# Chunked attention and two gated MLPs: attention and the second MLP's weight conversions spread at one distance into the last plain block, with the stores of weight high halves

## Chip, cores and metric

The kernel runs on one core of one Trainium2 chip. The metric is the device time in microseconds of one execution; lower is better.

## What is computed

Inputs are float32. Attention works in chunks of 64 tokens, then come two gated MLPs, the second behind an RMS norm. Its core:

```python
scores = scale * np.matmul(q_c, k_c.transpose(0, 1, 2, 4, 3))   # per chunk of 64 tokens
attn = np.exp(scores - np.max(scores, axis=-1, keepdims=True))
attn = attn / (np.sum(attn, axis=-1, keepdims=True) + 1e-09)
out = np.matmul(attn, v_c)                                      # 8 x 8 heads x 576 x 64
x = out.transpose(0, 2, 1, 3).reshape(4608, 512)
x = (silu(x @ w_gate) * (x @ w_val)) @ w_out                    # 512 -> 1536 -> 512
rms = np.sqrt(np.mean(x * x, axis=-1, keepdims=True) + 1e-06)
xn = x / rms * rms_g
out = (silu(xn @ w2_gate) * (xn @ w2_val)) @ w2_out
```

## The kernel before

**Precision.** Every float32 operand of a large product is split into a high part (rounded to the matmul's type) and a low part, and three matmuls make a product (`mm3`, L625): high by high, high by low, low by high. Weights arrive as words that are taken apart: `rebase` (two ScalarE steps, L124 and L131) and `to_f32` (two VectorE steps, L140 and L145) make a float32 tile.

**Stages.** The 4608 tokens are 36 tiles of 128. The first MLP runs 3584 tokens as seven plain blocks (0 to 6) of 512, and the last 1024 as a superblock that saves an eighth of its products by Strassen-Winograd sums; the second MLP is five such superblocks. A plain block has 12 iterations, one for each slice f of 128 hidden columns, 84 in all, numbered here from 0: block j has iterations 12j to 12j+11. An iteration issues on TensorE 12 matmuls for the gate (`emit_g`), 12 for the value (`emit_v`), 12 for the output of the slice before (`emit_y`). ScalarE takes the tanh and rounds the hidden slice (hh); VectorE makes the two products (sg) and the low part (hl). Gate and value have one PSUM bank each, so the next gate waits for the product that read the last one.

**Positions.** Everything else is hung between these by a table. An iteration n has three positions, 3n, 3n+1 and 3n+2: behind the gate, value and output matmuls. `put(l, j, pos, fn)` hangs a function on a position, and each engine runs its work in the order of issue. `NP` is 36, the positions of a block. For attention tile i (8 to 35) with a = `score_at(i)`: scores are made at a by `att_both(i-1)`, which issues the value matmuls of tile i-1 with them; `att_m` (maximum, 16 exponentials with sums) at a+1, `att_n` (reciprocal on VectorE, scaling on GpSimd) at a+2, `att_td` (eight VectorE transposes each) at a+3 and a+4, `trans_att(i+1)` (VectorE transposes of the next tile's q and k) at a+2. q and k come in groups of some two tiles, in four-row pieces that `spread` issues on SyncE over 11 positions.

**Conversions.** The second MLP's weights are converted in plain blocks 1 to 5: every 6 positions one slice of `w2` (load at +1, `rebase` at +4, `to_f32` at +6). With every second slice the Winograd sums of the pair follow on GpSimd (`comb_add`, `comb_rest`), ScalarE (`comb_cast`), and stores (`comb_keep`). Gate and value pairs and `LATE` = 2 of six output pairs are done so; the other four pairs are done by `late_o` in the first two superblocks: at steps 26 and 47 of the first (a step is one of the 84 pairs of kt products of its gate and value phase), and at 20 and 41 of the second. The first MLP's own sums for its superblock are made by `whole` and `first_add` in blocks 1 to 5, and `whole` also stores the high half of the weight. Low halves of the first MLP's weights are loaded anew in each block from ScalarE's queue (`load_lo`, `load_lo_o`, L191 and L198).

**Superblocks.** A superblock has six groups (fp) of 84 matmuls for gate and value and then an output phase; its weights come through a ring of 16 tiles (`load_ring`), its inputs through `x_load` and `x_prep`. `y_out` adds, transposes on VectorE and stores a quarter ("11", "22", "21", "12") of the output in pieces.

## Time and profile before

| | |
|---|---|
| median of 3 runs | 1817.12 us (1816.77 to 1818.37) |
| profiled execution | 1817.92 us, span 1816.1 us |
| TensorE busy | 1738.8 us, 96% |
| VectorE busy | 1278.0 us, 70% |
| ScalarE busy | 811.6 us, 45% |
| GpSimd busy | 548.9 us, 30% |
| DMA | 392.86 MB, mean 216 GB/s |

In the profile PE is TensorE, PEld its weight loads, DVE VectorE, ACT ScalarE, POOL GpSimd and SP SyncE. A name with q (SPq) is an engine's sequencer, which issues DMAs. An arrow in an instruction's name reads output <- inputs; in a wait, who waited <- what ended the wait. TensorE's busy share is an average over stages: 96% says little of a single block, for which the windows below are cut at the first gate matmul of a block.

### The profile page before, as it was taken

Reading aid. Unit: us, or ns where it says so; the run is one execution under the profiler, and the core shown is the slowest. Engines: PE = TensorE matmul, PEld = TensorE weight load, DVE = VectorE, ACT = ScalarE, POOL = GpSimd, SP = SyncE. Lnnn points to the kernel's source line nnn. Section 1 sums busy time; section 2 is a strip of 40 time slices with the busy share of each in tenths; the row PEclk is TensorE's granted clock in tenths of the full one; section 3 lists DMA queues with packets and bytes.
Section 4 is the critical chain, followed back from the end, with each engine's and each line's share of the span. In section 5 each row is a group of like instructions: output and inputs, shape, how many; then the busy total and the mean of one; then the engine's idle time right before and its main releaser. Section 6 shows DMA issues by size and latency. Waiting matters only on the chain.

```text
span 1816.1 us, 29440 instructions
## 1 busy us (share of the span) xinstructions
PE 1738.8 (96%) x9978; PEld 1452.0 (80%) x9978; DVE 1278.0 (70%) x2232; ACT 811.6 (45%) x1902; POOL 548.9 (30%) x527
## 2 busy tenths in 40 slices
PE   7998989999898999999999999999999999999998
PEld 5786777777776787888777777888888888999998
DVE  6985666777765768556879777874695569569566
ACT  6862433444334344334546444533462345345343
POOL 1003446556555474213351643110021011002000
PEclk9998999999999999999999999999999999999999
DMA  9994777778777777354673779687668767987986
GB/s 243 314 240 113 196 207 210 219 206 232 212 199 219 214 206 230 99 184 129 200 228 103 213 220 336 182 259 233 194 208 248 211 195 211 293 270 252 303 253 166
DMA packets 462533, 392.86 MB, mean 216 GB/s; under 512 B 278576, under 2 KB 334640, under 8 KB 462384
## 3 DMA queue, kind: packets, MB, share of 16 engines
q1 hardware_dynamic: 444368, 346.74, 65.5%
q10 hardware_dynamic: 18016, 44.24, 7.8%
q8 instruction: 80, 1.31, 0.3%
q14 instruction: 69, 0.57, 0.1%
HBM read 310.90 MB, written 79.95 MB: 215 GB/s over the span
## 4 chain that ended last, share of the span: by engine, by line
PE 60%; DVE 16%; DMA 11%; ACT 5%; issue 3%; SPq 3%; POOL 2%; ACTq 0%; DVEq 0%; POOLq 0%
DVE pT L536 4%; DMA l<-lo_scratch 3%; SPq L438 2%; PE g L626 2%; PE g L627 2%; PE g L628 2%; PE v L626 2%; DMA w64g<-in_moe_w_gate_dram 2%; ACT p L492 2%; PE v L628 2%; PE v L627 2%; DMA lo<-lo_scratch 1%; PE ygA L627 1%; PE ygA L628 1%; PE ygA L626 1%
## 5 line engine op out<-in xcount | busy, mean ns | idle before, releaser
L1073 POOL TENSOR_TENSOR h<-h,h 128x512 f32<-128x512 f32 (+1 forms) x36 | 46.4, 1290 | 526.3 <-DVE h L1051 526.3
L626 PE MATMUL g<-xh,wg 128*128 128x512 f32 x336 | 136.8, 407 | 21.1 <-DVE sg L639 19.2
L1109 DVE TENSOR_TENSOR hp<-h,hp 128x512 fp32r<-128x512 f32 (+1 forms) x216 | 147.3, 712 | 6.0 <-ACT hp L1108 5.9
L536 DVE STREAM_TRANSPOSE pT<-p 32x128 f32<-32x128 f32 x448 | 135.6, 303 | 16.1 <-POOL p L520 9.9
L1031 ACT ACTIVATE sig<-sgt 128x512 f32<-128x512 f32 (+1 forms) x108 | 64.5, 598 | 184.0 <-DVE sgt L1039 183.9
L1108 ACT CAST hp<-h 128x512 fp32r<-128x512 f32 (+1 forms) x216 | 121.6, 584 | 53.9 <-PE yvA L628 21.1
L626 PE MATMUL v<-xh,wv 128*128 128x512 f32 x336 | 134.0, 399 | 9.1 <-DVE sg L655 8.1
L970 POOL TENSOR_TENSOR xf<-xf,xf 128x512 f32<-128x512 f32 (+1 forms) x48 | 80.4, 1676 | 196.3 <-DVE xo0l L966 68.5
L1032 DVE TENSOR_TENSOR sgt<-sgt,sig 128x512 f32<-128x512 f32 (+1 forms) x108 | 73.7, 683 | 86.8 <-ACT sig L1031 86.8
L627 PE MATMUL g<-xl,wg 128*128 128x512 f32 x336 | 133.3, 397 | 0.4 <-DVE xl L620 0.4
L628 PE MATMUL g<-xh,l 128*128 128x512 f32 x336 | 133.4, 397 | 0.0
L520 POOL TENSOR_TENSOR p<-p,r 128x512 f32<-128x512 f32 x36 | 42.1, 1168 | 300.3 <-DVE r L519 279.0
L660 DVE TENSOR_TENSOR hl<-sg,hh 128x512 fp32r<-128x512 f32 x84 | 75.5, 899 | 81.1 <-ACT hh L658 80.7
L628 PE MATMUL v<-xh,l 128*128 128x512 f32 x336 | 131.1, 390 | 0.0
L627 PE MATMUL v<-xl,wv 128*128 128x512 f32 x336 | 131.0, 390 | 0.0
L658 ACT CAST hh<-sg 128x512 fp32r<-128x512 f32 x84 | 51.8, 616 | 156.6 <-DVE sg L655 147.5
L626 PEld LDWEIGHTS g<-xh,wg 128*128 128x128 f32 x336 | 64.5, 192 | 43.4 <-DVE sg L639 27.7
L639 DVE SCALAR_TENSOR_TENSOR sg<-sg,g 128x512 f32<-128x512 f32 x84 | 57.3, 682 | 48.2 <-ACT sg L638 47.9
L626 PEld LDWEIGHTS v<-xh,wv 128*128 128x128 f32 x336 | 63.0, 188 | 26.3 <-DVE sg L655 12.1
L638 ACT ACTIVATE sg<-g 128x512 f32<-128x512 f32 x84 | 50.1, 596 | 73.7 <-PE g L628 73.4
L627 PE MATMUL y<-hl,wo 128*128 128x512 f32 x168 | 68.8, 409 | 12.5 <-DVE hl L660 12.1
L1051 DVE TENSOR_TENSOR h<-h,sgt 128x512 f32<-128x512 f32 (+1 forms) x108 | 74.4, 689 | 3.7
(858 smaller groups left out, 5277.5 us busy)
## 6 DMA issues: line engine op xcount, KB each, us to landing
wrg<-w_scratch SPq DMA_DIRECT2D x210, 256.0 KB, 3.7
wrv<-w_scratch SPq DMA_DIRECT2D x210, 256.0 KB, 3.6
wro<-w_scratch SPq DMA_DIRECT2D x210, 256.0 KB, 3.2
l<-lo_scratch ACTq DMA_DIRECT2D x54, 512.0 KB, 4.3
lo<-lo_scratch ACTq DMA_DIRECT2D x60, 256.0 KB, 4.8
w64g<-in_moe_w_gate_dram SPq DMA_DIRECT2D x19, 512.0 KB, 5.1
w64v<-in_moe_w_val_dram SPq DMA_DIRECT2D x19, 512.0 KB, 4.6
w_scratch<-wsg SPq DMA_DIRECT2D x18, 512.0 KB, 3.1
```

What stands on the lines that cost most here:

```text
L536: nc.vector.transpose(out=pT[o:o + 32, :, r:r + 32], in_=pt[r:r + 32, :, z, b * 32:b * 32 + 32])
L626: nc.tensor.matmul(o, sh, mh, start=first, stop=False, skip_group_check=free)
L627: nc.tensor.matmul(o, sh, ml, start=False, stop=False, skip_group_check=free)
L628: nc.tensor.matmul(o, sl, mh, start=False, stop=last, skip_group_check=free)
L639: return sg, lambda: nc.vector.scalar_tensor_tensor(out=sg[:, :n], in0=sg[:, :n], scalar=1.0, in1=g[:, :n], op0=ALU.add, op1=ALU.mult)
L660: return product, lambda: nc.vector.tensor_sub(hl[:, :n], sg[:, :n], hh[:, :n].bitcast(F32))
L970: nc.gpsimd.tensor_sub(o, a, b)
L1031: nc.scalar.activation(sg[:, :tw], src[:, :tw], AF.Sigmoid)
L1032: nc.vector.tensor_mul(t[:, :tw], src[:, :tw], sg[:, :tw])
L1051: nc.vector.tensor_mul(h[:, :tw], src[:, :tw], sgt[pos][:, :tw])
L1108: nc.scalar.copy(hh[:, :tw], src)
L1109: nc.vector.tensor_sub(hl[:, :tw], src, hh[:, :tw].bitcast(F32))
```

## The change

- Attention tiles come every 7 positions instead of 6.75 on the average, conversions every 7 instead of 6. So the last tile's value matmuls stand at position 232, in iteration 77, instead of 225, in iteration 75; the last conversion's sums reach position 230.
- `rebase` stands 4 positions behind its load instead of 3, `trans_att` of the next tile at a+5 instead of a+2, and the pieces of a q and k group start 3 positions later.
- The high halves are stored by `high_keep` in block 6, in 36 stores at positions 0 to 23, instead of by `whole` in blocks 1 to 5.
- `LATE` is 1: a fifth output pair goes to the superblocks; the first now has three, at steps 10, 31 and 52.
- The input of the first superblock is prepared from iteration 79 on, two pieces at each position, instead of from iteration 77, four at the end of each iteration.
- The RMS sums of a block are made at other positions, other tiles stand last, held stores are let go at two of three steps instead of one of two, and half of the "21" stores of the last superblock go out from ScalarE's queue.

```diff
--- before.py
+++ after.py
@@ -200,7 +200,7 @@
 
     flat = {}
     NP2 = NF // 2
-    LATE = 2
+    LATE = 1
     HK = KD * P // 2
     comb = {}
 
@@ -266,6 +266,9 @@
         h = whi[0, nm, f]
         nc.gpsimd.tensor_add(t, h.bitcast(F32), low_of(0, j, chunk(j, f), nm).bitcast(F32))
         flat[0, nm, f] = t
+
+    def high_keep(nm, p, side):
+        h = whi[0, nm, 2 * p + side]
         ks = [(k, c) for k, (which, c) in enumerate(PLAIN[nm]) if which == side]
         k, c, n = ks[0][0], ks[0][1], len(ks)
         nc.sync.dma_start(
@@ -308,7 +311,7 @@
 
     NCH = NT // CH
     SC = S // CH
-    last = [33, 34, 35, 12, 13, 22, 23, 24]
+    last = [12, 13, 22, 23, 32, 33, 34, 35]
     home = [i for i in range(NT // P) if i not in last] + last
     order = [home.index(i) for i in range(NT // P)]
 
@@ -794,7 +797,7 @@
             put(l, j, pos + z, lambda z=z: step(z))
 
     def score_at(i):
-        return NP + 27 * (i - 8) // 4
+        return NP + 7 * (i - 8)
 
     for i in range(NW // P, NT_):
         j = order[i] * P // NW
@@ -806,11 +809,11 @@
                 put(0, 0, a, lambda: att_both(7))
                 put(0, 0, a - 1, lambda: trans_att(8))
             put(0, 0, a + 1, lambda i=i: att_m(i))
-            if i + 1 < NT_:
-                put(0, 0, a + 2, lambda i=i: trans_att(i + 1))
             put(0, 0, a + 2, lambda i=i: att_n(i))
             put(0, 0, a + 3, lambda i=i: att_td(i, 0))
             put(0, 0, a + 4, lambda i=i: att_td(i, 1))
+            if i + 1 < NT_:
+                put(0, 0, a + 5, lambda i=i: trans_att(i + 1))
             put(0, 0, e, lambda i=i: att_both(i))
             put(0, 0, e + 1, lambda i=i, j=j: att_lo(i, j))
         else:
@@ -827,7 +830,7 @@
             g = where[c][0]
             if g > 0 and c == groups[g][-1] and g + 2 < len(groups):
                 if i > 8:
-                    dq, dv, nq, nv = score_at(i - 1) + 3, score_at(i + 1) + 1, 11, 4
+                    dq, dv, nq, nv = score_at(i - 1) + 6, score_at(i + 1) + 1, 11, 4
                 else:
                     dq, dv, nq, nv = {4: (20, 17, 9, 3), 6: (29, 38, 8, 4), 8: (38, 44, 11, 4)}[i]
                 spread(0, 0, dq, nq, lambda g=g: load_qk(g + 2))
@@ -838,9 +841,10 @@
             put(0, j, 3 + 2 * d, lambda pj=pj, d=d: rms_sq(pj, d))
         put(0, j, 13, lambda pj=pj: rms_cast(pj))
         put(0, j, 14, lambda pj=pj: rms_split(pj))
-        put(0, j, 17, lambda pj=pj: rms_mm(pj))
-        put(0, j, 20, lambda pj=pj: rms_mul(pj))
-        put(0, j, 22, lambda pj=pj: rms_newton(pj))
+        mm = (17, 17, 17, 16, 20, 19)[j - 1]
+        put(0, j, mm, lambda pj=pj: rms_mm(pj))
+        put(0, j, mm + 2, lambda pj=pj: rms_mul(pj))
+        put(0, j, mm + 4, lambda pj=pj: rms_newton(pj))
         for d in range(KD):
             put(0, j, 24 + 2 * d, lambda pj=pj, d=d: rms_x(pj, d))
             put(0, j, 26 + 2 * d, lambda pj=pj, d=d: rms_keep(pj, d))
@@ -849,13 +853,13 @@
 
     w2 = [(nm, f) for nm, m in (("g", NP2), ("v", NP2), ("o", LATE)) for fp in range(m) for f in (fp, fp + NP2)]
     for x, (nm, f) in enumerate(w2):
-        pos = NP + 6 * x
+        pos = NP + 7 * x
         put(0, 0, pos + 1, lambda nm=nm, f=f: load_w64(1, nm, f))
-        put(0, 0, pos + 4, lambda nm=nm, f=f: rebase(1, nm, f))
-        put(0, 0, pos + 6, lambda nm=nm, f=f: to_f32(1, nm, f))
+        put(0, 0, pos + 5, lambda nm=nm, f=f: rebase(1, nm, f))
+        put(0, 0, pos + 7, lambda nm=nm, f=f: to_f32(1, nm, f))
         if f >= NP2:
             for d, fn, kk in COMB:
-                put(0, 0, pos + d, lambda fn=fn, nm=nm, f=f, kk=kk: fn(nm, f - NP2, kk))
+                put(0, 0, pos + 1 + d, lambda fn=fn, nm=nm, f=f, kk=kk: fn(nm, f - NP2, kk))
 
     w1_at = (
         (1, 4, "g"), (1, 2, "g"), (1, 0, "g"),
@@ -874,6 +878,10 @@
                 put(0, j, a + 4 + d, lambda nm=nm, p=p, kk=kk: first_add(nm, p, kk))
             for kk in kept:
                 put(0, j, a + 4 + d, lambda nm=nm, p=p, kk=kk: first_keep(nm, p, kk))
+
+    for f in range(NF):
+        for z, nm in enumerate("gvo"):
+            put(0, NB - 1, 2 * f + z // 2, lambda nm=nm, f=f: high_keep(nm, f // 2, f % 2))
 
     ORDER = (0, 1, 4, 3, 5, 2, 6)
     GV = [(m, k) for k in ORDER for m in "gv"]
@@ -1152,7 +1160,7 @@
         for a, (x, n, r) in [(a, run) for a in range(0, P, 32) for run in rows(r0, tw)]:
             dst = out[r:r + n, c0 + a:c0 + a + 32].rearrange("(b t) d -> t b d", t=32)
             src_ = o[a:a + 32, x:x + n].rearrange("t (b d) -> t b d", d=32)
-            queue = nc.scalar if s == len(SB) - 1 and pos == "12" and a >= 64 else nc.sync
+            queue = nc.scalar if s == len(SB) - 1 and pos in ("12", "21") and a >= 64 else nc.sync
             if slow:
                 held.append((dst, src_))
             else:
@@ -1405,12 +1413,16 @@
             def run(p):
                 for fn in at.get(3 * n + p, ()):
                     fn()
+                if j == NB - 1 and f >= 7:
+                    for _ in range(2):
+                        if xops:
+                            xops.pop(0)()
 
             head = (l, j) == (0, 0)
             if (j, f) == (1, 0):
                 conv.close()
                 cv = open_pool(conv, "cv2", 2, "right")
-            if (j, f) == (NB - 1, 4):
+            if (j, f) == (NB - 1, 6):
                 conv.close()
                 attn.close()
                 X2 = open_pool(two, "x2", 1, "right")
@@ -1428,9 +1440,8 @@
                 nc.sync.dma_start(out=rg, in_=moe2_rms_g.rearrange("(c p) -> p c", p=P))
             if head and f in (2, 5):
                 issue(load_tok(6 + f // 5))
-            if (j, f) == (NB - 1, 8):
+            if (j, f) == (NB - 1, 9):
                 x_load(0, 1)
-            if (j, f) == (NB - 1, 9):
                 load_ring(16)
                 xops = xops + x_prep(0, 1)
             if prev is not None:
@@ -1461,10 +1472,6 @@
                 if not f:
                     conv1(5)
                 conv1(3 * f + 6)
-            if j == NB - 1 and f >= 5:
-                for _ in range(4):
-                    if xops:
-                        xops.pop(0)()
             prev = (l, j, f)
         lo()
 
@@ -1484,7 +1491,7 @@
         when(late, 17, rms_mm, pj, True)
         when(late, 20, rms_mul, pj)
         when(late, 22, rms_newton, pj)
-        for fp, (t, n) in zip(range(LATE, NP2), ((late, 26), (late, 47), (norm, 20), (norm, 41))):
+        for fp, (t, n) in zip(range(LATE, NP2), ((late, 10), (late, 31), (late, 52), (norm, 20), (norm, 41))):
             for d, fn in late_o(fp).items():
                 when(t, n + d, fn)
         for z in range(2):
@@ -1518,7 +1525,7 @@
                     if (s, fp, z) != (0, 0, 0):
                         gv_after(s, fp, m, kk, banks)
                         load_ring(wn + 16)
-                        flush(z % 2)
+                        flush(1 if z % 3 else 0)
                     for fn in extra.get(s, {}).get(14 * fp + z, ()):
                         fn()
                     ring_split(wn + 7)
```

The order of VectorE at the end of iteration 12 and in iteration 13. qT9 and kT9 are the transposed q and k of tile 9, pT8 the probabilities of tile 8, sg0_1_1 the products of block 1, slice 1, hl0_1_0 the low part of slice 0. Before:

```order
L449 STREAM_TRANSPOSE qT9_1876<-xq_4_1567 128x512
L449 STREAM_TRANSPOSE kT9_1878<-xk_4_1568 128x512
L519 RECIPROCAL r8_1840<-r8_1840 128x8
L660 TENSOR_TENSOR hl0_1_0_1835<-sg0_1_0_1798,hh0_1_0_1834 128x512
L536 STREAM_TRANSPOSE pT8_1907<-p8_1838 32x4x32 x8
L639 SCALAR_TENSOR_TENSOR sg0_1_1_1900<-sg0_1_1_1900,g0_1_1_1887 128x512
L536 STREAM_TRANSPOSE pT8_1907<-p8_1838 32x4x32 x8
L655 SCALAR_TENSOR_TENSOR sg0_1_1_1900<-v0_1_1_1921,sg0_1_1_1900 128x512
L660 TENSOR_TENSOR hl0_1_1_1935<-sg0_1_1_1900,hh0_1_1_1934 128x512
```

With the change:

```order
L522 RECIPROCAL r8_1840<-r8_1840 128x8
L663 TENSOR_TENSOR hl0_1_0_1835<-sg0_1_0_1798,hh0_1_0_1834 128x512
L539 STREAM_TRANSPOSE pT8_1903<-p8_1838 32x4x32 x8
L642 SCALAR_TENSOR_TENSOR sg0_1_1_1896<-sg0_1_1_1896,g0_1_1_1883 128x512
L539 STREAM_TRANSPOSE pT8_1903<-p8_1838 32x4x32 x8
L658 SCALAR_TENSOR_TENSOR sg0_1_1_1896<-v0_1_1_1917,sg0_1_1_1896 128x512
L452 STREAM_TRANSPOSE qT9_1966<-xq_4_1567 128x512
L452 STREAM_TRANSPOSE kT9_1968<-xk_4_1568 128x512
L663 TENSOR_TENSOR hl0_1_1_1931<-sg0_1_1_1896,hh0_1_1_1930 128x512
```

The two transpositions moved from the head of this piece to behind the second product.

The order of ScalarE around the first step (crv10_1) of the conversion of value slice 10. hh is the rounded hidden slice that TensorE reads, p27 and r27 are the exponentials of tile 27, l and lo loads of low halves. Before, in iterations 55 and 56:

```order
L492 ACTIVATE p27_6509,r27_6511<-both_26_6446,m27_6508 128x64 x8
L496 ACTIVATE r27_6511<-r27_6511 128x8
L237 CAST wsv3_2_6554<-crv9_1_6118 128x256
L124 ACTIVATE crv10_1_6556<-w64v10_1_6430 128x512
L131 ACTIVATE cmv10_1_6557<-w64v10_1_6430 128x512
L658 CAST hh0_4_7_6540<-sg0_4_7_6498 128x512
```

With the change, in iteration 62:

```order
L237 CAST wsv3_2_7062<-crv9_1_6649 128x256
L661 CAST hh0_5_2_7079<-sg0_5_2_7043 128x512
L124 ACTIVATE crv10_1_7120<-w64v10_1_7000 128x512
L131 ACTIVATE cmv10_1_7121<-w64v10_1_7000 128x512
L641 ACTIVATE sg0_5_3_7140<-g0_5_3_7127 128x512
L191 DMA l_0_5_5_7142<-lo1_scratch_59 128x1024
```

The step stood between the exponentials and the rounding of the same iteration; now the rounding is ahead of it, and the next tanh behind it.

The end of ScalarE's program; hp are rounded hidden slices, yo the transposed output. Before:

```order
L1108 CAST hp39_5_18892<-h22_3_5_18077 128x384
L1108 CAST hp40_5_18907<-h22_4_5_18241 128x384
L1108 CAST hp41_5_18910<-h22_5_5_18423 128x384
L1159 DMA out_0_dram<-yo012_5_18977 32x12x32 x2
L1159 DMA out_0_dram<-yo112_5_18991 32x12x32 x2
L1596 UNCONDITIONAL_BRANCH
```

With the change:

```order
L1116 CAST hp41_5_18921<-h22_5_5_18434 128x384
L1167 DMA out_0_dram<-yo021_5_18930 32x8x32
L1167 DMA out_0_dram<-yo021_5_18930 32x4x32
L1167 DMA out_0_dram<-yo021_5_18930 32x8x32
L1167 DMA out_0_dram<-yo021_5_18930 32x4x32
L1167 DMA out_0_dram<-yo121_5_18946 32x8x32
L1167 DMA out_0_dram<-yo121_5_18946 32x4x32
L1167 DMA out_0_dram<-yo121_5_18946 32x8x32
L1167 DMA out_0_dram<-yo121_5_18946 32x4x32
L1167 DMA out_0_dram<-yo012_5_18988 32x12x32 x2
L1167 DMA out_0_dram<-yo112_5_19002 32x12x32 x2
```

Eight stores of the "21" quarter came to ScalarE's queue from SyncE's.

## Rows read from the trace of the kernel before

**Rows 1.** Windows (us, busy us by engine, clock, DMA share): two iterations; blocks 1 to 6.

```profile
174.68:182.84 8.16, 8.16 (x38) 6.76 (x36) 7.54 (x20) 1.10 (x2) 7.48 (x8) 1.00 0.71 189
182.84:192.32 9.48, 9.48 (x102) 7.71 (x100) 5.61 (x9) 4.70 (x12) 3.47 (x5) 1.00 0.71 181
137.80:265.48 127.68, 113.43 (x788) 90.67 (x786) 79.37 (x167) 48.56 (x166) 48.28 (x51) 0.93 0.62 165
265.48:382.70 117.22, 109.71 (x756) 85.04 (x755) 79.56 (x167) 48.85 (x158) 70.16 (x77) 1.00 0.79 221
382.70:501.65 118.95, 110.59 (x756) 87.75 (x754) 85.91 (x176) 49.18 (x158) 67.19 (x71) 0.97 0.76 214
501.65:624.38 122.73, 112.60 (x819) 88.79 (x818) 80.45 (x166) 51.83 (x176) 62.01 (x67) 0.97 0.77 214
624.38:734.79 110.41, 106.90 (x756) 85.72 (x754) 81.86 (x173) 48.81 (x159) 63.62 (x70) 1.00 0.71 207
734.79:835.39 100.60, 100.60 (x532) 82.88 (x530) 52.20 (x82) 30.38 (x64) 24.61 (x18) 1.00 0.44 142
```

**Rows 2.** Waits of PE, blocks 1 to 5: line <- releaser: us, times, longest.

```profile
PE g L626 <- DVE sg L639: 19.2, 18, 2.9
PE y L627 <- DVE hl L660: 11.5, 10, 7.1
```

**Rows 3.** Windows: iteration 13.

```profile
146.82:164.57 17.75, 10.69 (x38) 8.32 (x36) 6.55 (x17) 2.43 (x4) 5.22 (x5) 0.75 0.43 103
```

**Rows 4.** Timeline near iteration 13 (start, us, idle before): VectorE, SyncE, ScalarE.

```profile
156.37 0.71 DVE L449 STREAM_TRANSPOSE qT<-xq 128x512 f32<-128x512 f32 x1 [8.04 <-DMA xq<-in_q_dram]
...
140.28 14.47 SPq L438 DMA_DIRECT2D xq<-in_q_dram  x4
...
149.87 0.34 ACTq L191 DMA_DIRECT2D l<-lo_scratch  x1
```

**Rows 5.** Waits of ScalarE and of SyncE, blocks 1 to 5.

```profile
ACT crg L124 <- DMA w64g<-in_moe_w_gate_dram: 47.4, 9, 10.9
ACT crv L124 <- DMA w64v<-in_moe_w_val_dram: 36.0, 7, 6.3
...
SPq L438 <- DMA l<-lo_scratch: 108.5, 31, 12.7
```

**Rows 6.** Windows: iterations 44 and 45; 52 to 56.

```profile
459.98:485.20 25.22, 20.02 (x138) 15.27 (x136) 17.00 (x31) 9.07 (x31) 16.06 (x17) 0.93 0.77 215
538.59:595.52 56.93, 47.68 (x311) 36.79 (x311) 34.54 (x75) 22.52 (x66) 28.15 (x33) 0.97 0.81 230
```

**Rows 7.** Timeline: ScalarE in iteration 56.

```profile
587.78 0.66 ACT L124 ACTIVATE crv<-w64v 128x512 f32<-128x512 f32 x1 [5.69 <-DMA w64v<-in_moe_w_val_dram]
```

**Rows 8.** Windows: iterations 46 to 51; 28 to 33.

```profile
485.20:538.59 53.39, 52.50 (x351) 42.21 (x345) 37.28 (x79) 22.56 (x83) 24.80 (x26) 1.00 0.73 199
304.40:363.20 58.80, 54.91 (x352) 42.12 (x346) 40.37 (x84) 27.01 (x88) 29.52 (x33) 1.00 0.79 217
```

**Rows 9.** Windows: first superblock, third to fifth group.

```profile
877.94:942.51 64.57, 58.90 (x253) 46.79 (x253) 52.13 (x72) 32.46 (x76) 34.28 (x36) 1.00 0.72 229
```

**Rows 10.** Lines (count | busy us, mean ns): groups three to five; last row group six.

```profile
L243 POOL TENSOR_TENSOR lws<-lwt,lws 128x256 fp32r<-128x256 f32 x8 | 7.4, 933 | 0.0
...
L1089 DVE TENSOR_TENSOR t<-h,h 128x512 f32<-128x512 f32 x3 | 3.1, 1033 | 0.0
...
L1089 DVE TENSOR_TENSOR t<-h,h 128x512 f32<-128x512 f32 x2 | 1.4, 684 | 0.0
```

**Rows 11.** DMA issues: count, KB each, median us to landing.

```profile
xf<-x_scratch SPq DMA_DIRECT2D x8, 256.0 KB, 3.7
```

**Rows 12.** Timeline of the end: VectorE, SyncE.

```profile
1811.61 0.58 DVE L1149 STREAM_TRANSPOSE yo<-yt 128x384 f32<-128x384 f32 x1 [2.67 <-DMA out_dram<-yo]
...
1796.56 16.48 SPq L1159 DMA_DIRECT2D out_dram<-yo  x28
```

## Prediction

> **What bounds the kernel now.** First the stretches of the program, cut at the first gate matmul of each plain block [rows 1]. An iteration without attention takes 8.16 us, one with the score and value matmuls of a tile 9.48 us, so a tile costs 1.32 us. A block of 12 iterations would take 97.9 us and its tiles. Blocks 1 to 5 have 6 (the first without value matmuls, about 0.7 us), 5, 5, 6 and 5 tiles and take 127.7, 117.2, 119.0, 122.7 and 110.4 us; what is over is 22.5, 12.7, 14.4, 16.9 and 5.9 us, together 72.4 us. Block 6 takes 100.6 us with two part tiles, 0.6 us over. So most of the loss lies in the five blocks that carry attention and conversions, and block 6 is almost free: VectorE is busy there 52 us of 101, against 80 to 86 us in blocks 2 to 5. In the waits of TensorE in that stretch [rows 2] VectorE comes first: TensorE waits for the product that frees a PSUM bank, or for hl, the low part of the hidden slice. Yet VectorE is idle for a quarter to two fifths of each block, so it isn't short of speed: it stands in order behind something that is late. TensorE's own idle time in blocks 1 to 5 (length less busy) is 14.3, 7.5, 8.4, 10.1 and 3.5 us, 43.8 in all. The other 29 us of the 72.4 are matmuls at a lower clock: around the longest stop the granted clock is 0.75 instead of 1.00 [rows 3]. A stop that goes takes its slow matmuls with it.
>
> **Part A, tile 9.** The longest stop is in iteration 13, 17.75 us long [rows 3], 9.6 over. VectorE is idle for 8.04 us in front of the transposition of tile 9's q [rows 4], whose transfer is late: SyncE spent 14.47 us on four issues, and went on after ScalarE had issued a weight load at 149.87 (the two queues share their DMA semaphores, and an issue waits for the DMA that last used its semaphore). The hl that TensorE needs stands behind the transposition. In the changed order the transposition stands behind hl, both transposes of the probabilities and the second product. The iteration begins at 146.8 and its gate and value matmuls take 5.4 us, so VectorE comes to it at about 153 instead of 148 us. It then still waits for the transfer, till 156.4, but what stands behind it is needed only in the next iteration, which begins at 155: the next hl after its gate and value matmuls, about 160.4, and the product that frees the gate's bank at its end, about 164. I take 9 us of the 9.6.
>
> **Part B, ScalarE in front of a weight load.** ScalarE stands idle in front of the first conversion step of a gate or value weight, for its load, 83.4 us in 16 waits [rows 5]. Whether TensorE feels it depends on what stands behind. Iterations 44 and 45 take 25.22 us with one tile, 7.6 over, and 52 to 56 take 56.93 with two, 13.5 over [rows 6]: 21.1 us in two places that hold five such waits. In the last of them ScalarE begins at 587.78 after 5.69 us [rows 7], and hh, which TensorE needs, stands behind. The change puts the step one position later behind the same load. A position is 8.16 / 3 = 2.7 us, and in the order hh stands ahead of the step at that place now. Five waits shorter by 2.7 us are 13.6 us; I take 14.
>
> **Part C, the rest.** 72.4 - 9.6 - 21.1 = 41.7 us are left over 180 positions, 25.7 periods of seven, so 1.6 us per period. Before, a tile came every 6.75 positions and a conversion every 6, so their distance drifted. Now both come every 7, at a fixed distance: scores and the end of the last conversion at 0, exponentials at 1, the transposes of the probabilities at 3 and 4, those of q and k at 5, with the first step of the new conversion. Two stretches of the old trace had nearly this distance [rows 8]: iterations 46 to 51 take 53.39 us, 1.8 over for six iterations and two tiles, or 0.7 per seven positions; iterations 28 to 33 take 58.80 us, 7.2 over, or 2.8. These are the bounds. The second lies in the block with most work on GpSimd (70 us), and 36 stores of high halves now leave blocks 1 to 5, so I stay nearer to the first: 1.1 per period over 27 periods, 30 us, a gain of 12. The ends are +34 (2.8 times 27, less 41.7) and -23 us. The stores land in block 6, where the DMA share is 0.44, and I cost them at nothing; without that cover they are 36 issues on SyncE, for which nothing in that block waits.
>
> **Part D, the added conversion.** A pair of output weights moves from the plain blocks into the first superblock, which now has three pairs (from steps 10, 31 and 52) instead of two (26 and 47). Three groups of 84 matmuls take 64.57 us there [rows 9]; where nothing waits they take 19.04 each (84 matmuls, when 36 take 8.16). So 7.4 us are over for two conversions, 3.7 each. I take +4. The lower end is +1, as the last steps fall into a group that had no loss and has some cover; the upper is one conversion's whole work on GpSimd, eleven operations of which eight took 7.4 us for two [rows 10], 0.93 each, 10.2 us.
>
> **Part E, the hand-over.** The first superblock's input is prepared two iterations later, six pieces per iteration instead of four. Its second load goes out in the iteration that first uses it and lands after 3.7 us [rows 11], where 2.7 us of gate matmuls cover it. I take +1, ends 0 and +4.
>
> **Part F, the end.** The last transposition waits 2.67 us for the store that last used its buffer, since SyncE issues 28 stores in one row of 16.48 us [rows 12]. Half of the 16 stores of the "21" quarter now leave from ScalarE's queue, which has no other work then. I take -2.6, ends -1 and -2.7. The new positions of the RMS steps, the flush rate and the new order of the last eight tiles move single instructions by a position; I cost them at nothing, since they move into gaps of the same iteration, and at 1 us either way if that cover is gone.
>
> **Sum.** -9 - 14 - 12 + 4 + 1 - 2.6 = -32.6 us on the profiled execution's 1817.9 us gives 1785.3. That execution lies 0.8 us over the median of the three runs, inside their spread. I predict 1785 us.
>
> **A rule against this.** VectorE's difference t of two SBUF tiles takes 1.03 us in the groups with a conversion and 0.68 us in the next group, without one [rows 10]: 0.35 us dearer, which the 3.7 us per conversion already hold. The Trainium skill, "SBUF — State Buffer", section "Who interferes with whom", says that a VectorE instruction with two SBUF inputs and a GpSimd one that reads SBUF exclude each other, and the later one waits until the other is through. By that rule the added conversion would cost up to its whole 10.2 us on GpSimd, and the sum would be 1791.5.
>
> **Rivals.** (1) **Most stops go.** If the fixed distance behaves as in iterations 46 to 51 and part B's 21.1 us vanish, A to C give -9.6 - 21.1 - 23 = -53.7, with +2.4 of D to F -51.3, and the time is 1767. For it: block 6 and those six iterations; against it: ScalarE's waits are many and long. (2) **The wait moves along.** SyncE stands 108.5 us for ScalarE's loads [rows 5]; if it only gets later with the conversion's step, B and C give between nothing (-9 + 2.4, 1811 us) and half (-13 more, 1798 us). (3) **The clash repeats, slower.** q and k are now transposed two positions (5.4 us) ahead of the score matmuls that read them, instead of four or five. Their transposes take 1.4 us, so TensorE stops in every tile as soon as VectorE is 4 us late there. If each period then loses 2.8 us, as in iterations 28 to 33, C becomes +34, B keeps half (-7), and the sum is -9 - 7 + 34 + 2.4 = +20.4: 1838 us. It is slower where C costs more than 13.6 us, that is from 2.05 us per period on. Against it: VectorE has 38 us idle even in block 2. (4) **VectorE stands for GpSimd in the superblock**, at each operation of the conversion in full: 10.2 for 4 us in D, 1791.5 us, as above.
>
> **How the numbers follow.** About 0.2% (3.6 us) is what can be told from no change. My forecast, 1774 to 1796, gets 0.45; rival 1 0.18; rival 4 0.09; rival 2 0.13; rival 3 0.09; and 0.06 that gains and costs cancel within 0.2%. Faster is 0.45 + 0.18 + 0.09 + 0.13 = 0.85. The range goes from 1762, a little under rival 1, to 1810, the upper end of rival 2; it leaves out the slower case, no change, and little below. The likeliest case's own range is 1774 to 1796.
>
> **What would show it.** Right: iteration 13 near 9.5 us; blocks 1 to 6 over by some 40 us instead of 73; ScalarE's waits for gate and value loads together below 50 us; the first superblock longer by 4 us; no wait of the last transposition. Wrong: TensorE waiting in the score matmuls for qT or kT (rival 3); waits for those loads as long as before (rival 2); a first superblock longer by 10 us (rival 4).

## The result, and the profile after

The changed kernel takes 1786.93 us (median of 4 runs, 1785.77 to 1788.23), the kernel before 1817.74 beside it (1816.77 to 1819.05): a ratio of 0.983, 95% interval 0.9813 to 0.9847. The profiled execution took 1788.23 us, its span is 1786.5, against 1816.1. All times below that come from a trace are compared as spans.

Windows of the changed kernel, with the columns of [rows 1]: iteration 13, then blocks 1 to 6.

```profile
146.60:154.76 8.16, 8.16 (x37) 6.76 (x36) 6.18 (x18) 1.19 (x2) 6.29 (x6) 1.00 0.22 71
...
137.59:249.28 111.69, 109.08 (x787) 88.55 (x785) 76.88 (x164) 44.50 (x145) 50.05 (x52) 0.97 0.62 164
249.28:363.89 114.61, 108.62 (x762) 87.03 (x755) 76.92 (x161) 48.68 (x157) 59.51 (x64) 0.99 0.75 206
363.89:471.36 107.47, 105.92 (x756) 85.96 (x755) 75.34 (x163) 50.45 (x170) 60.84 (x67) 1.00 0.72 202
471.36:581.88 110.52, 107.33 (x756) 87.17 (x755) 76.18 (x157) 45.95 (x149) 57.80 (x61) 0.98 0.74 204
581.88:689.57 107.69, 105.98 (x756) 85.88 (x754) 81.70 (x176) 49.41 (x159) 61.02 (x68) 1.00 0.77 219
689.57:793.33 103.76, 103.00 (x595) 83.44 (x594) 62.70 (x110) 38.78 (x97) 34.11 (x30) 1.00 0.67 223
```

Each iteration is again set against 8.16 us and 1.32 for a whole tile. By that measure, which is called **over** from here on, the six blocks were 22.5, 12.7, 14.4, 16.9, 5.9 and 0.7 us over before, 73.1 together, and are 6.5, 10.1, 2.9, 6.0, 3.2 and 2.5 over now, 31.3 together. That is 41.8 us less. Iteration 13 has no stop left [rows 3].

The waits of TensorE, ScalarE and SyncE from block 1's start to 735 us, where block 5 ended before, answer to [rows 2, 5]:

```profile
PE g L629 <- DVE sg L642: 3.5, 4, 1.6
PE ssq L738 <- POOL al L727: 3.1, 1, 3.1
PE y L630 <- DVE hl L663: 2.1, 3, 1.5
...
ACT crg L124 <- DMA w64g<-in_moe_w_gate_dram: 41.2, 7, 12.1
ACT crv L124 <- DMA w64v<-in_moe_w_val_dram: 11.8, 5, 6.8
...
SPq L441 <- DMA l<-lo_scratch: 92.5, 31, 14.5
```

TensorE's waits for VectorE are nearly gone (19.2 us in 18 waits are 3.5 in 4, 11.5 in 10 are 2.1 in 3). ScalarE's waits for gate and value loads are 53.0 us instead of 83.4, and the longest is longer. (The two queues share DMA semaphores, so a wait can bear the name of a neighbouring DMA; this matters in one run below.) Of what is left, three stops make 17.7 us: 6.4 over in iteration 17, 5.7 in 33, 5.6 in 53. The first two stand in the timeline of ScalarE:

```profile
186.32 0.66 ACT L124 ACTIVATE crg<-w64g 128x512 f32<-128x512 f32 x1 [10.40 <-DMA w64g<-in_moe_w_gate_dram]
...
337.05 0.66 ACT L124 ACTIVATE crg<-w64g 128x512 f32<-128x512 f32 x1 [12.13 <-DMA w64g<-in_moe_w_gate_dram]
```

The superblocks hold one term that was seen and one that was not. The windows show the whole first superblock and the first group of the last one, first before, then with the change; below them are the waits of TensorE and VectorE in that group, with the change.

```profile
835.39:1024.45 189.06, 179.30 (x771) 143.14 (x770) 159.72 (x242) 105.33 (x226) 73.92 (x61) 1.00 0.57 176
1677.13:1691.69 14.56, 14.56 (x85) 14.56 (x85) 7.02 (x14) 4.12 (x9) 0.00 (x0) 1.00 1.03 305
...
793.33:986.25 192.92, 182.24 (x771) 143.91 (x770) 161.10 (x240) 108.07 (x233) 82.25 (x72) 0.99 0.60 187
1639.28:1664.29 25.01, 17.47 (x86) 17.15 (x86) 7.35 (x14) 4.30 (x10) 0.00 (x0) 0.80 0.72 211
...
PE p0gA L629 <- ACT s2g L1031: 7.5, 1, 7.5
...
DVE yo L1157 <- DMA wrg<-w_scratch: 8.4, 1, 8.4
DVE yo L1157 <- DMA out_dram<-yo: 4.6, 1, 4.6
```

The first superblock took 189.06 us before, so it is 3.9 us longer. The first group of the last one took 14.56 and takes 25.01, 10.45 more: VectorE stands for buffers of output slices, ScalarE's copy s2g behind it, and TensorE behind that. The end is shorter: from TensorE's last matmul to the end of the span 5.53 us instead of 7.81. The timeline there shows the last transposition without a wait and SyncE's row of stores cut from 28 to 20 [rows 12]:

```profile
1781.57 0.58 DVE L1157 STREAM_TRANSPOSE yo<-yt 128x384 f32<-128x384 f32 x1
...
1769.15 13.86 SPq L1167 DMA_DIRECT2D out_dram<-yo  x20
```

The sum closes: -0.2 ahead of block 1, -41.8 in the plain blocks, +3.9 and +0.3 in the first two superblocks, +10.45 in the last one's first group, -2.3 at the end make -29.65, and the spans differ by 29.6.

### The profile page after: what moved, and what is told of

Read it like the earlier page. It is cut to its first block, busy times and chain, and to the rows that moved or that the text cites. A ratio compares the mean times of both kernels' runs of the same rounds, so it can differ in the third digit from the quotient of the medians.

```text
span 1786.5 us, 29482 instructions
## 1 busy us (share of the span) xinstructions
PE 1731.0 (97%) x9978; PEld 1452.7 (81%) x9978; DVE 1269.8 (71%) x2232; ACT 813.9 (46%) x1902; POOL 544.9 (31%) x527
## 4 chain that ended last, share of the span: by engine, by line
PE 70%; DVE 11%; DMA 9%; ACT 3%; issue 3%; SPq 2%; POOL 1%; ACTq 0%; DVEq 0%; POOLq 0%
PE g L629 3%; PE g L630 3%; PE g L631 3%; PE v L629 3%; PE v L630 2%; PE v L631 2%; DMA l<-lo_scratch 2%; DVE pT L539 2%; PE y L629 1%; PE ygA L630 1%; PE ygA L629 1%; PE yvA L631 1%; PE yvA L630 1%; PE yvA L629 1%; PE ygA L631 1%
## 5 line engine op out<-in xcount | busy, mean ns | idle before, releaser
L663 DVE TENSOR_TENSOR hl<-sg,hh 128x512 fp32r<-128x512 f32 x84 | 71.6, 853 | 24.0 <-ACT hh L661 23.4
L631 PEld LDWEIGHTS g<-xh,l 128*128 128x128 f32 x336 | 63.1, 188 | 13.9 <-DVE l L171 0.4
```

Of the source, the lines that this page charges most:

```text
L631: nc.tensor.matmul(o, sl, mh, start=False, stop=last, skip_group_check=free)
L663: return product, lambda: nc.vector.tensor_sub(hl[:, :n], sg[:, :n], hh[:, :n].bitcast(F32))
```

## Experiments

Each is compared with the kernel before that ran beside it on the same chip, 1814 to 1816 us in the median; the changed kernel has 0.983 by the same measure.

**Transposition early again.** In the changed kernel:

```diff
-                put(0, 0, a + 5, lambda i=i: trans_att(i + 1))
+                put(0, 0, a + 2, lambda i=i: trans_att(i + 1))
```

> The changed kernel with the next tile's q and k transposed at a+2 again, ahead of the probabilities, all else as changed. Theory (part A: the transposition stands in front of hl while its transfer is late): iteration 13 is again about 17.7 us instead of 8.2, and a few other groups whose transfer is late show the same, so 1796 to 1800 us (+9 to +13). Rival (the equal distance of tiles and conversions did it, not the place of the transposition): iteration 13 under 10 us and 1787 us within 3.

Measured: 1806.24 us (1803.11 to 1809.74), ratio 0.9948 (0.9933 to 0.9963). The six blocks are 21.7, 5.2, 9.3, 0.5, 10.3 and 2.1 over, 49.2 together instead of 31.3. Iteration 13 has its old stop, as its window shows, and 9.6 of the 17.9 us are there:

```profile
148.11:165.84 17.73, 10.68 (x37) 8.30 (x36) 6.54 (x17) 1.19 (x2) 5.22 (x5) 0.75 0.42 103
```

So part A is real, and it is needed at other tiles too: VectorE waits 44.4 us in front of transpositions of q and k up to 800 us, against 1.9 in the changed kernel. The largest of these waits:

```profile
DVE kT L455 <- DMA xv<-in_v_dram: 17.8, 3, 7.2
...
DVE qT L452 <- DMA xk<-in_k_dram: 8.1, 1, 8.1
```

**The first conversion step early again.**

```diff
-        put(0, 0, pos + 5, lambda nm=nm, f=f: rebase(1, nm, f))
+        put(0, 0, pos + 4, lambda nm=nm, f=f: rebase(1, nm, f))
```

> The changed kernel with the first conversion step 4 positions behind its load again instead of 5, all else as changed. Theory (part B: ScalarE waits for the load with hh behind it): ScalarE's waits for w64g and w64v grow from about 55 to 80 us and more, and the time by 10 to 14 us, to 1797 to 1801. Rival (at an equal distance the wait has nothing behind it that TensorE needs): the waits grow as much, but the time stays at 1787 us within 3.

Measured: 1789.28 us (two runs, 1788.26 and 1790.3), ratio 0.9865 (0.9845 to 0.9885), an interval that still touches the changed kernel's; the blocks are 30.6 over. ScalarE's waits in front of the first step of gate and value weights, up to 735 us:

```profile
ACT crg L124 <- DMA w64g<-in_moe_w_gate_dram: 36.3, 7, 10.7
...
ACT crv L124 <- DMA w64v<-in_moe_w_val_dram: 18.1, 4, 6.9
ACT crg L124 <- DMA xv<-in_v_dram: 11.0, 1, 11.0
...
ACT crv L124 <- DMA xk<-in_k_dram: 9.5, 1, 9.5
```

The two waits that are put down to loads of v and k ended within 0.1 us of the landing of the weight load itself, so they belong to the sum: 74.9 us, against 53.0 in the changed kernel (54.7 counted in the same way). The waits grew by 20 us, and the plain blocks lose no more. The rival's outcome came, and part B's mechanism falls: a shorter wait gains nothing when it ends at the same time. One step shows it, first in the changed kernel, where block 1 begins at 137.59, then in this run, where it begins at 139.09:

```profile
161.01 0.68 ACT L124 ACTIVATE crg<-w64g 128x512 f32<-128x512 f32 x1 [4.13 <-DMA w64g<-in_moe_w_gate_dram]
...
162.62 0.66 ACT L124 ACTIVATE crg<-w64g 128x512 f32<-128x512 f32 x1 [10.99 <-DMA xv<-in_v_dram]
```

It starts 23.4 us into the block and 23.5, after 4.1 us of waiting and after 11.0. The rival's reason, that TensorE needs nothing behind the wait, is not shown. A step every seven positions falls on an iteration's three positions in turn, so in both kernels hh comes next, ahead of the next tanh, behind 17 of the 26 steps, and only 9 have hh ahead of them.

**The transposition later, alone**, in the kernel before:

```diff
-                put(0, 0, a + 2, lambda i=i: trans_att(i + 1))
+                put(0, 0, a + 5, lambda i=i: trans_att(i + 1))
```

> The kernel before with one part of the change alone: the next tile's q and k transposed at a+5 instead of a+2. Theory (part A stands by itself): iteration 13 about 8.2 us instead of 17.75, total 1808 us (-9), with up to 4 us more where other transfers were late. Rival 3 (transposes so near to the score matmuls make TensorE wait in each tile): waits of the score matmuls for qT or kT appear, and the time is 1817 us or more.

Measured: 1832.76 us (two runs, 1828.96 and 1836.57), ratio 1.0105 (1.0076 to 1.0134), slower. Iteration 13 is free (window), but the blocks are 89.7 over, since SyncE waits for the transposition (7.3 us before; waits up to 735 us):

```profile
146.87:155.03 8.16, 8.16 (x37) 6.76 (x36) 6.17 (x18) 1.19 (x2) 6.29 (x6) 1.00 0.21 69
...
SPq L438 <- DVE qT L451: 43.2, 5, 16.3
```

The load of the group after next reuses the buffer that the transposition reads. Left at its old position, it now stands in SyncE's queue ahead of that transposition, with the weight loads behind it: ScalarE's waits for gate and value weights grow to 108.9 us. Rival 3's sign appears as well: TensorE waits 9.5 us in the score matmuls for the transposed k, most of it in the line below, where the changed kernel has no such wait.

```profile
PE both L466 <- DVE kT L449: 8.3, 5, 2.7
```

**The transposition and the group loads later**, in the kernel before: the edit above and

```diff
-                    dq, dv, nq, nv = score_at(i - 1) + 3, score_at(i + 1) + 1, 11, 4
+                    dq, dv, nq, nv = score_at(i - 1) + 6, score_at(i + 1) + 1, 11, 4
```

> The kernel before with two parts of the change: the transposition of q and k three positions later, and the loads of the next group three positions later too, so that no load stands in SyncE's queue ahead of the transposition that frees its buffer. Theory (part A gains only with the later loads): SyncE's waits for the transposition fall from 43 us, with the transposition alone, to below 10; iteration 13 stays free of its stop; the other blocks stay as before, 73.1 - 9.6 = 63 over; the time is 1802 to 1809. Rival (the later transposition itself stops TensorE and ScalarE at the old spacing): over by 80 or more, 1825 to 1835.

Measured: 1824.52 us (1817.79 to 1827.88), ratio 1.0048 (1.0032 to 1.0063). SyncE's wait for the transposition fell, but ScalarE's waits for weights did not:

```profile
SPq L438 <- DVE qT L451: 10.5, 3, 5.0
...
ACT crg L124 <- DMA w64g<-in_moe_w_gate_dram: 64.7, 9, 10.6
ACT crv L124 <- DMA w64v<-in_moe_w_val_dram: 31.1, 6, 10.0
```

The blocks are 80.4 over, 7 more than before, and TensorE waits 10.1 us in the score matmuls for the transposed k. So the rival holds: by itself part A, done whole, loses. With all else of the change in place it gains 18; which other part it needs, the spacing or another, was not tried alone.

**Tiles every 6.75 positions again**, conversions every 7:

```diff
-        return NP + 7 * (i - 8)
+        return NP + 27 * (i - 8) // 4
```

> The changed kernel with the tiles every 6.75 positions again, conversions still every 7. Theory (part C: a fixed distance between tiles and conversions spares stops): the distance drifts over the 27 conversions, stops return where the two meet badly; blocks 1 to 6 are over by 38 to 45 us instead of 31.3, the time is 1793 to 1801. Rival (it is the wider spacing of the conversions, 7 for 6, that gains, not the fixed distance): over by 28 to 35, the time within 4 us of the changed kernel's 1787.

Measured: 1810.24 us (1805.95 to 1816.41), ratio 0.9979 (0.9961 to 0.9998). The blocks are 4.4, 14.9, 6.3, 15.3, 10.0 and 2.2 over, 53.0 together. The direction is the theory's, the size about twice that: a quarter position per tile takes back half of what the plain blocks had gained.

**Every conversion three positions later**, at a distance as fixed, but another one:

```diff
-        pos = NP + 7 * x
+        pos = NP + 3 + 7 * x
```

> The changed kernel with every conversion three positions later, so that its distance to the tiles is as fixed as in the changed kernel, but another one. Theory (what spares stops is that no bad meeting comes round, so most fixed distances do): blocks 1 to 6 over by 25 to 38 us (31.3 in the changed kernel), 1781 to 1794. Rival (it is this distance that is good; the drifting one passes through better and worse, 53 over on the average): 45 to 75 over, 1800 to 1830.

Measured: 1825.0 us (1822.27 to 1826.93), ratio 1.0059 (1.0038 to 1.008); 68.3 over. The rival holds: a fixed distance is not enough. The shift also moves the conversions against the first MLP's sums and the RMS steps, whose positions stay, so it isn't shown that the distance to the tiles is the one that counts. The worst stop is iteration 34, 12.3 over; the waits in it:

```profile
PE y L629 <- ACT hh L661: 5.1, 1, 5.1
...
ACT crg L124 <- DMA w64g<-in_moe_w_gate_dram: 9.5, 1, 9.5
...
POOL wav L267 <- DMA w_scratch<-wag: 17.3, 1, 17.3
```

Both the weight load that ScalarE waits for and the store that GpSimd waits for are issued by SyncE. Why they are later in this order wasn't taken apart further.

**High halves stored where they are added up**, as before:

```diff
         flat[0, nm, f] = t
+        ks = [(k, c) for k, (which, c) in enumerate(PLAIN[nm]) if which == side]
+        k, c, n = ks[0][0], ks[0][1], len(ks)
+        nc.sync.dma_start(
...
-            put(0, NB - 1, 2 * f + z // 2, lambda nm=nm, f=f: high_keep(nm, f // 2, f % 2))
```

> The changed kernel with the high halves stored again where the halves are added up, in blocks 1 to 5, instead of in block 6. Theory (as the prediction costed part C: 36 stores fewer on SyncE's queue spare waits behind them): SyncE's waits for GpSimd's and ScalarE's loads grow, blocks 1 to 5 are over by 5 to 15 us more than 28.8, block 6 by up to 2 less; the time is 1790 to 1800. Rival (the stores cost nothing in either place): within 2 us of 1787.

Measured: 1803.96 us (1796.14 to 1807.44), ratio 0.9935 (0.9908 to 0.9962). Blocks 1 to 5 are 42.7 over instead of 28.7, block 6 2.3 instead of 2.5. So 36 stores fewer on SyncE are worth 14 us, and in block 6 they cost nothing. The waits of iteration 53, which is now 10.0 over, show the way from a late store to TensorE:

```profile
PE ssq L744 <- POOL al L733: 7.0, 1, 7.0
...
POOL wao L267 <- DMA w_scratch<-wao: 10.6, 1, 10.6
```

**The last eight tiles in another order**, in the changed kernel:

```diff
-    last = [12, 13, 22, 23, 32, 33, 34, 35]
+    last = [32, 33, 34, 35, 12, 13, 22, 23]
```

> The changed kernel with the same eight tiles last but in the order 32 to 35, 12, 13, 22, 23, so that the fifth superblock of the second MLP's two halves lie in one run of rows each. Theory (the changed order broke a half into two runs, so 40 held stores instead of 24, and the last superblock's first group waits 10.4 us for their buffers): that group takes 14.6 us again instead of 25.0; the last quarter's stores are then two runs instead of one, 1 to 2 us later at the end; 1778 us (1776 to 1780). Rival (the new rate at which held stores are let go is at fault, or the stores' place in the queue): the first group stays near 25 us, 1787 us.

Measured: 1779.39 us (1775.57 to 1782.32), ratio 0.9808 (0.9787 to 0.9828). The group that took 25.01 us takes 14.56 again, and the end from the last matmul on 8.0 instead of 5.5:

```profile
1638.99:1653.55 14.56, 14.56 (x85) 14.56 (x85) 7.02 (x15) 4.21 (x9) 0.00 (x0) 1.00 1.04 316
```

In the changed order the second half of the fifth of the six superblocks is tile 31 and tiles 12 and 13, two row runs of the output, and so 40 held stores instead of 24; here it is 31 to 33, one run.

**ScalarE's loads of the low parts first.**

```diff
-            sg, product = emit_g(l, j, f)
             if NF <= n + 2 < len(iters):
                 load_lo(*iters[n + 2])
             if n >= NF:
                 load_lo_o(*iters[n])
+            sg, product = emit_g(l, j, f)
```

> The changed kernel with ScalarE's loads of the low weight parts issued ahead of the gate's matmuls and tanh in the order, instead of behind. Theory (SyncE's 92.5 us in 31 waits in front of the q, k, v and weight loads are for ScalarE's loads, with which it shares DMA semaphores; an earlier issue ends them earlier): those waits fall below 60 us, ScalarE's waits for gate and value weights below 45, blocks 1 to 6 are over by 22 to 28 instead of 31.3; the time is 1778 to 1784. Rival (the waits only hide others, the stops at iterations 17 and 33 have the slow transfer itself as their cause): over by 29 to 34, 1784 to 1790.

Measured: 1772.41 us (1768.34 to 1773.07), ratio 0.9759 (0.974 to 0.9779). The blocks are 3.3, 6.9, 0.5, 4.0, 0.5 and 1.2 over, 16.5 together. The waits of SyncE and ScalarE up to the end of block 6:

```profile
SPq L441 <- DMA l<-lo_scratch: 98.0, 34, 9.3
...
ACT crg L124 <- DMA w64g<-in_moe_w_gate_dram: 30.5, 6, 7.7
ACT crv L124 <- DMA w64v<-in_moe_w_val_dram: 4.3, 2, 4.0
```

The time went below what was expected and ScalarE's waits fell as expected, but SyncE's sum did not fall (98.0 us against 92.5, longest 9.3 instead of 14.5). Iterations 17, 33 and 53 are 2.6, under 1.5 and 2.7 over instead of 6.4, 5.7 and 5.6. The chain that leads to the first of these stops in the changed kernel shows how such a load acts:

```profile
166.90 2.48 ACT p L495 x16
...
169.55 4.48 DMA l<-lo_scratch
174.04 0.31 SPq L441
...
181.29 5.01 DMA w64g<-in_moe_w_gate_dram
```

A load of l goes out behind the exponentials, SyncE stands until it has landed, and the weight load stands behind that. In this run the same load goes out at 167.59 instead of 169.55, the weight load at 179.49 instead of 181.29, and the chain there holds no load of l. Sums of waits do not tell what a plain block loses: SyncE's is as large as before, and ScalarE's for gate and value loads is 32.6 us in the shifted version, which is 68.3 over, and 74.9 in the one with the step early, which is 30.6 over.

**Two combined versions.** Both have the low-part loads first and block 4's RMS matmul at 20 instead of 16. The first also has the order 32 to 35, 12, 13, 22, 23; the second keeps the changed order and lets its stores go faster:

```diff
-                        flush(1 if z % 3 else 0)
+                        flush(2 if s == len(SB) - 1 else 1 if z % 3 else 0)
...
-                    flush(2)
+                    flush(4 if s == len(SB) - 2 else 2)
```

> ScalarE's loads of the low parts ahead of the gate's matmuls (the version that took 1772.4 us), with two more edits: the last eight tiles in the order 32 to 35, 12, 13, 22, 23, and block 4's RMS matmul at position 20 instead of 16. Theory (held stores stop the last superblock's first group, the early RMS matmul stops iteration 53): that group falls from 24.8 to 14.6 us, the end after the last matmul grows from 5.5 to 8, iteration 53 is 0 to 0.5 over instead of 2.7; 1772.4 - 10.2 + 2.5 - 2.5 = 1762 us, 1759 to 1765. Rival (the RMS matmul stops as long at its new place, or stops another iteration): 1764 to 1768.

> As the run before, but with the changed kernel's own order of the last eight tiles, and its 40 held stores let go four at a time in the fifth superblock's output groups and two per step in the last superblock. Theory (the hold-back, not the number of stores, stops the group): the group falls to 15 to 17 us, the end stays at 5.5; 1772.4 - 8.5 - 2.5 = 1761, 1758 to 1764. Rival (SyncE can't issue 24 stores at 0.59 us in the 12 us in which their buffers are wanted again): the group still takes 19 to 24 us, or the output groups of the fifth superblock get longer; 1764 to 1770.

Measured: 1766.63 us (1764.72 to 1771.02), ratio 0.9746 (0.9724 to 0.9769), and 1768.16 (1762.62 to 1769.82), ratio 0.9742 (0.9719 to 0.9765): equal within their intervals, and faster than both kernels; by the ratio neither is clearly faster than the loads first alone (0.9759). Both lie above the ranges expected for them (to 1765 and to 1764), in their rivals' ranges. The first one's rival came, iteration 53 stops as long; the second one's did not, the group is near what was expected. Windows of the last superblock's first group in the first version, then of its first and second in the other:

```profile
1625.35:1639.90 14.55, 14.55 (x85) 14.55 (x85) 7.01 (x14) 4.11 (x9) 0.00 (x0) 1.00 1.01 293
...
1625.73:1641.57 15.84, 14.85 (x86) 14.53 (x86) 7.03 (x14) 4.11 (x9) 0.00 (x0) 1.00 0.80 206
1641.57:1658.72 17.15, 15.61 (x86) 14.43 (x85) 7.77 (x15) 5.03 (x11) 1.01 (x1) 1.00 0.88 247
```

With one run fewer the stop is gone, and the end takes 7.0 us; with faster release 3.9 of 10.45 us are left, and the end takes 5.5. The RMS matmul's place did nothing: iteration 53 is 2.5 over, against 2.7 with the loads first alone. Its waits in the first combined version show TensorE standing for hl instead, while GpSimd stands for the same store:

```profile
PE y L630 <- DVE hl L663: 1.5, 1, 1.5
...
POOL wao L267 <- DMA w_scratch<-wao: 7.8, 1, 7.8
```

## Why the prediction was right, and where it was not

1785 us was forecast, 1786.9 came. Its total is better than its steps: against the -32.6 us of the sum the profiled executions differ by -29.7, and in that part C gained 7 us more than written while the new order of the last tiles cost 10.45 that were costed at nothing. That these nearly cancel is luck.

- **Part A (-9): shown, and by its own working.** In the changed kernel's timeline of iteration 13 SyncE still stands (16.27 us for four issues) and q's transposition begins at 156.33, as late as before, but hl is ahead of it:

```profile
148.14 0.64 DVE L663 TENSOR_TENSOR hl<-sg,hh 128x512 fp32r<-128x512 f32 x1
...
156.33 0.71 DVE L452 STREAM_TRANSPOSE qT<-xq 128x512 f32<-128x512 f32 x1
...
138.24 16.27 SPq L441 DMA_DIRECT2D xq<-in_q_dram  x4
```

  Iteration 13 lost its 9.6 us. What the step left out is that the gain hangs on the rest of the diff: alone, and with only the later group loads beside it, the same move cost 17 and 7 us in the plain blocks.
- **Part B (-14): right in size by luck, wrong in cause.** Iterations 44, 45 and 52 to 56 were 21.1 over [rows 6] and are 6.2 over, 14.9 less; but they hold other conversions now. The sentence "Five waits shorter by 2.7 us are 13.6 us" fails: with the step at its old place the waits are 20 us longer, and the blocks stay at 30.6 over. What counts is when the load lands, not when ScalarE begins to wait. "In the order hh stands ahead of the step at that place now" holds for 9 of 26 steps, among them the one that was shown; before, hh came behind all 28. The steps of the stops in iterations 17 and 33 are among the 17 that still have hh behind them.
- **Part C (-12): inside its bounds, the gain larger than written.** The rest, 42.4 us with block 6's 0.7, is 25.1; with the 1.8 us by which block 6 grew, put down to part E, C gave 19.1. The bounds from two stretches at nearly this distance [rows 8], 0.7 and 2.8 us per period, held it: 25.1 us over 27 periods are 0.9. The reason given for staying near the lower one, 36 stores fewer on SyncE, is shown: 14 us. That the place of the conversions counts is shown as well, by 22 us for a drift and 37 for a shift by three; that the distance to the tiles is what counts is not.
- **These three terms are not separate.** Undoing the transposition, the spacing or the stores alone costs 18, 22 and 14 us in the plain blocks, 54 of a gain of 41.8. The lateness also changes its place: with the transposition early VectorE waits 42 us more for q and k, and ScalarE's waits for gate and value weights fall to 13.7 us by name, 23.6 with those named after neighbours, from 53.0. That all this is one late queue, SyncE's, is likely but was not measured.
- **Part D (+4): right,** 3.9. Rival 4 falls: the superblock did not grow by the added conversion's whole 10.2 us on GpSimd. That was the prediction's price for the rule of the Trainium skill, "SBUF — State Buffer", section "Who interferes with whom", that a VectorE instruction with two SBUF inputs and a GpSimd one that reads SBUF exclude each other. For single instructions the trace agrees with that rule: hl's subtraction, which has two SBUF inputs, takes at most 0.69 us where no GpSimd instruction runs beside it and up to 1.79 where one does, while the first product, with one input from PSUM, never takes more than 0.69. What fell is the assumption that every operation on GpSimd is paid for in full.
- **Part E (+1): 1.8** more in block 6, which holds it beside other moved work; **part F (-2.6): -2.3.** Both inside their ends.
- **"The new positions of the RMS steps, the flush rate and the new order of the last eight tiles": the step that failed.** Costed at nothing, within 1 us, the order cost 10.45. It decides how many row runs an output half has and so how many stores are held; the flush rate, raised from a half to two thirds per step, did not keep up with 40 instead of 24. Of the RMS positions only block 4's was moved back, in the combined versions, and that gained nothing.
- **"The other 29 us of the 72.4 are matmuls at a lower clock": misread.** The clocks of [rows 1], 0.93, 0.97 and 0.97 in blocks 1, 3 and 4 and 1.00 in 2 and 5, make about 16 us. Block 2 is busy 5.2 us too long at 1.00. No term of the sum uses the 29; what the rest is stays open.
- **Signs.** The first superblock and the last transposition came as written, iteration 13 took 8.16 us instead of the 9.5 written; 31 us are over instead of 40; ScalarE's waits stayed at 53, just above the 50 named. Rival 2 said that part B's wait would only move along: the single step gained nothing, and the time still fell, for the other reasons.

## What to carry to other kernels

Where two engines' DMAs are queued so that one stands for the other's transfers, price a change of order on that queue as a whole: list which loads and stores it moves past which wait, since parts that look separate may gain only together, and one alone may lose. A wait that gets shorter is worth nothing if it ends at the same time; ask what makes its end earlier. Count the output's stores, too: an order of tiles that splits a half into two row runs doubles its stores, and with held buffers that is a stop. And try to issue a load ahead of the compute that shares its queue: here that was worth 14.8 us in the plain blocks, as much as 36 stores moved away.

## What the runs showed that was not expected

- **A place in a queue costs time without a byte more.** Two loads issued ahead of one group of matmuls and its tanh instead of behind halved what was left over (31.3 to 16.5 us), with the same bytes and the same number of DMAs.
- **A stop costs more than its wait.** In the last superblock's first group TensorE waits 7.5 us in its longest wait, and the group is 10.45 us longer: its matmuls are busy 17.47 us instead of 14.56. The mean granted clock is 0.80 there, and 1.00 when the wait is gone. In the combined version the mean granted clock of the span is 0.998, against 0.991 in the changed kernel.
- **A quarter position per tile** (0.7 us) undoes 22 us of the gain in the plain blocks, and a fixed shift by three positions 37, so a schedule of this kind has to be judged at its exact positions.
